# First batch in chunks of 64 tokens, and a pair's scores and sums in one block of products

## The chip, the cores and the metric

The kernel runs on one core of a Trainium2 chip. The metric is the time of one execution in device microseconds (us), as the median of five runs. All matrices are 32-bit floats; in the profile each product (matmul) leaves two records, with one weight load each.

## What is computed

Retention attention, then a two-layer network with a parametric ReLU:

```python
q, k, v: (8 batches, 8 heads, 576 tokens, 64)
scores = q @ k.T / sqrt(64)
Dmat = where(t >= s, gamma[h] ** (t - s), 0)      # gamma[h] = 1 - 2 ** (-5 - h)
ret = (scores * Dmat) @ v
x = ret as (8 * 576 tokens, 8 * 64)               # 4608 x 512
h = x @ w_in                                      # 512 x 2048
g = max(h, 0) + alpha * min(h, 0)
out = g @ w_out                                   # 2048 x 512
```

## The kernel before

Attention is computed in chunks. Within a chunk, the scores of each query with the keys are masked and multiplied with the values; all earlier chunks come in through a 64x64 matrix per head, the running sum of keys times values, which is multiplied with the queries ("the carried sums"). The powers of gamma are folded into scaled copies of q and v.

**The network** works on blocks of 256 tokens (`kb`) and units (`i`, eight per block, 256 of the 2048 hidden features each). Blocks 0 and 1 are "plain": `plain_unit` (L429) makes a unit's hidden values in the PSUM bank psh0, ACT takes them out with two ReLUs (L433, L435), DVE joins the two (L445, in `plain_relu`), and `plain_out` (L408, called by `mlp_out`) makes four products of 128x512 with w_out. `mlp_out` takes the oldest unit of the list `pend`; in the loop of the second batch that is the unit before. psh0 has one buffer, so the next L429 waits until L445 has read it. The later blocks (2 to 17) use a scheme with seven products in place of eight (`mlp_unit`, L473, and L391).

**The weights** come in 32 pieces of 512 KB, four per unit (two of w_in, two of w_out). `piece_in` takes a piece on ACT (L299, L301), `piece_out` works on it with three DVE operations (L310, L313, L315) and one on POOL (L317). Loads run ahead on SP's queue, limited by the bytes in flight (`load`, L78), and a loaded piece frees the buffer of a later one.

**The first batch** stands in three parts: tokens 0 to 255, 256 to 511 (the two large parts) and 512 to 575 (the last). For each large part, in this order: POOL scales q and v (`part_scale`, L678), TensorE transposes k and q (`part_transposes`, L698), then come the scores (`part_scores`, L719), the masks (`part_masks`: half of them one DVE operation, L729, the other half an ACT copy L731 and a POOL operation L732), the sums (`part_states`, L746; taken out by ACT L752 and POOL L754, or by DVE L756), the values and carried sums (`part_values`, L772 and L781), and ACT's copies to xb (L786). Chunks are 128 tokens long, two per part. Three products that nobody reads (`idle`, L849) follow the first part. The last part has its own functions (`last_transposes` L794, `last_scores` L803, `last_values` L814 and L821).

**The second batch** has four pairs of heads (n = 4 to 7), with nine chunks of 64. Its steps lie between the twelve plain units n = 0 to 11 that are left (i from 2 to 7, kb 0 and 1). `gap()` takes the next step at two places of a unit: ahead of `mlp_out`, and behind the second `piece_in`. The steps of a pair: "s" scores (`pair_scores`, L562, with masks L570 on DVE), "u" key-value products (`pair_states`, L580) with their running sums (`running_sums`, L589 on ACT, L591, L595, L597 on DVE), "w" their copies into the value tile (L603) and "p" the scaling of the next pair (L534 on POOL, L539 on ACT), "v" values (`pair_values`, L655, and ACT's L666) and "t" the next pair's transposes (L545 on DVE). `combine` adds weight sums on POOL (L327).

From L135 to L954 the order is the program's own (`tc.manual_schedule()`): each engine does its instructions in the order in which the code issues them. **The third batch and later** use `joint`: a pair's values are followed at once by `pair_front` for the next pair, which issues the scores (L619) and the key-value products (L625) as one block into two shared banks, and the ninth chunk's scores (L975) into a bank of its own, `extra`, masked by L632; the other masks are L639.

Of the kernel before, what the change touches and what calls it, by code (L numbers as in the profile page):

```python
# [14 lines left out]
ALU = mybir.AluOpType  # L15
# [3 lines left out]
def kernel(  # L19
# [121 lines left out]
    def room(i, s0, n):  # L141
# [8 lines left out]
        ((5, 4), (5, 5)), ((6, 5), (6, 6)))]  # L150
    carry = [None] + [room(i, 6, 1).rearrange("p (c d) -> p c d", d=D) for i in (2, 7)]

    def load_part(x):
        j0, j1 = PARTS[x]
        for i, src in ((0, k), (1, q), (2, v)):
            for m in range((j1 - j0 + 1) // 2):
# [5 lines left out]
                else:  # L162
# [20 lines left out]
    mask2 = const.tile([P, P], FP32, name="mask2")  # L183
    nc.gpsimd.memset(mask2, 1.0)
    nc.gpsimd.affine_select(out=mask2, in_=mask2, compare_op=ALU.is_ge, fill=0.0, base=0,
                            pattern=[[1, P]], channel_multiplier=-1)

    def mask(to):

        return mask2[to, to.start:to.stop]  # L190

# [208 lines left out]
    def plain_out(kb, i, g, between):  # L400
# [3 lines left out]
        for x in range(2):  # L404
            if x and between:
                between()
            for m in range(2):
                nc.tensor.matmul(acc[kb][m], g[:, 2 * x + m],  # L408
                                 w_out[i][:, 2 * x:2 * x + 2].rearrange("p x f -> p (x f)"),
                                 start=(i == 0 and x == 0), stop=(i == NU - 1 and x == 1))  # L410
# [140 lines left out]


    def pair_scores(n, kT, qT):
        c = pairs[n][1]

        mt = attn.tile([P, 2 * S], FP32, tag="at", name=f"mt_{n}").rearrange(
            "p (h j s) -> p h j s", h=2, s=C)
        ps = [ps_tile([P, NM, C], f"ps{p2}_{n}") for p2 in range(2)]
        for j in range(NJ):
            for h2 in range(2):  # L560
                x = (1 - h2, h2)[j % 2]
                nc.tensor.matmul(ps[j % 2][half(x), j // 2], kT[half(h2), chunk(j)],  # L562
                                 qT[half(h2), chunk(j)], start=True, stop=True)
        for h2 in range(2):
            nc.scalar.copy(mt[half(h2), h2].rearrange("p j s -> p (j s)"), qT[half(h2)])
        for p2 in range(2):
            for h2 in range(2):
                h, to, x = 2 * c + h2, half(1 - h2), (1 - h2, h2)[p2]
                nm = NM - p2
                nc.vector.scalar_tensor_tensor(  # L570
                    out=mt[to, h2, p2::2], in0=ps[p2][half(x), 0:nm], scalar=th[to, 3, h:h + 1],
                    in1=mask(to)[:, None, :].to_broadcast([C, nm, C]), op0=ALU.mult, op1=ALU.mult)
        return mt

    def pair_states(n, kn, vn):
        ps = [ps_tile([P, NM - 1, D], f"pu{p2}_{n}") for p2 in range(2)]
        for j in range(NJ - 1):
            for h2 in range(2):
                x = (h2, 1 - h2)[j % 2]
                nc.tensor.matmul(ps[j % 2][half(x), j // 2], kn[half(1 - h2), j],  # L580
                                 vn[half(1 - h2), h2, j], start=True, stop=True)
        return running_sums(n, *ps)

# [22 lines left out]

    later = []

    def pair_front(n, kT, qT, kn, vn, extra):
# [20 lines left out]
        for h2 in range(2):  # L630
            to = half(1 - h2)
            nc.vector.scalar_tensor_tensor(  # L632
                out=mt[to, h2, NJ - 1], in0=extra[to],
                scalar=th[to, 3, 2 * c + h2:2 * c + h2 + 1], in1=mask(to),
                op0=ALU.mult, op1=ALU.mult)
        for p2 in range(2):
            for h2 in range(2):
# [4 lines left out]
                    in1=mask(to)[:, None, :].to_broadcast([C, NM - 1, C]),  # L642
                    op0=ALU.mult, op1=ALU.mult)
        later.append(lambda: pair_sums(vn, running_sums(n, ps[0][:, 1], ps[1][:, 1])))
# [62 lines left out]

    def part_scores(x):
        at = tat[x] = [(mlp.tile([P, 8 * P], FP32, tag="g", name=f"pa{h2}_{x}") if x == 0 or h2
                        else room(4, 0, 4)).rearrange("p (c s) -> p c s", c=NPAIR)  # L710
                       for h2 in range(2)]
        banks = part_banks(x, 2 if x == 0 else None, "ps0"), part_banks(
            x, None if x == 0 else 0, "ps1")
        kT, qT = tT[x, 0], tT[x, 1]
        for m in range(2):
            to = slice(m * P, (m + 1) * P)
            for c in range(NPAIR):
                for h2 in range(2):
                    nc.tensor.matmul(banks[h2][m][:, c * P:(c + 1) * P], kT[half(h2), c, to],  # L719
                                     qT[half(h2), c, to], start=True, stop=True)  # L720
        return banks

    def part_masks(x, banks, h2):
        for m in range(2):
            to = tat[x][h2][:, :, m * P:(m + 1) * P]
            fro = banks[h2][m].rearrange("p (c s) -> p c s", c=NPAIR)
            w = mask2[:, None, :].to_broadcast([P, NPAIR, P])
            if h2 == 0:
                nc.vector.tensor_tensor(out=to, in0=fro, in1=w, op=ALU.mult)  # L729
            else:  # L730
                nc.scalar.copy(to, fro)  # L731
                nc.gpsimd.tensor_tensor(out=to, in0=to, in1=w, op=ALU.mult)  # L732

    def part_bank(x, n, b):
        return (ps_o.tile([P, 4 * P], FP32, tag=f"pso{n}", name=f"{b}_{x}") if n is not None else
                ps_a.tile([P, 4 * P], FP32, tag="psa", name=f"{b}_{x}"))


    def part_states(x):
        kn, vn = part[x][0], part[x][2]  # L740
        u = part_bank(x, 0 if x == 0 else None, "pu").rearrange("p (m c d) -> p m c d", m=2,
                                                                c=NPAIR)
        for m in range(2):
            for c in range(NPAIR):
                for h2 in range(2):
                    nc.tensor.matmul(u[half(h2), m, c], kn[:, m, 2 * c + h2],  # L746
                                     vn[:, m, 2 * c + h2], start=(m == 0 and c == 0),
                                     stop=(m == 1 and c == NPAIR - 1), skip_group_check=True)
        was = carry[x]
        for m in range(2):  # L750
            if x == 0:
                nc.scalar.copy(sums[x][m], u[:, m])  # L752
                if m:
                    nc.gpsimd.tensor_tensor(out=sums[x][m], in0=was, in1=sums[x][m], op=ALU.add)  # L754
            else:
                nc.vector.tensor_tensor(out=sums[x][m], in0=was, in1=u[:, m], op=ALU.add)  # L756
            was = sums[x][m]

    def part_carry(x):
        nc.gpsimd.tensor_tensor(out=carry[x + 1], in0=sums[x][1],  # L760
                                in1=gch[:, 2, :, None].to_broadcast([P, NPAIR, D]), op=ALU.mult)

    def part_values(x):
        vn, qT, at = part[x][2], tT[x, 1], tat[x]
        banks = [part_bank(x, (1, 2)[m] if x == 0 else (None, 2)[m], f"pv{m}").rearrange(
            "p (c s) -> p c s", c=NPAIR) for m in range(2)]
        xb[x] = ring.tile([P, NCC, TB], FP32, tag=f"x{x}", name=f"xb_{x}")
        su = [carry[x], sums[x][0]]
        for h2 in range(2):
            for m in range(2):  # L770
                for c in range(NPAIR):
                    nc.tensor.matmul(banks[m][half(h2), c], vn[:, m, 2 * c + h2],  # L772
                                     at[h2][:, c, m * P:(m + 1) * P], start=(c == 0),
                                     stop=(su[m] is None and c == NPAIR - 1),
# [266 lines left out]
```

## Time and profile before

| | |
|---|---|
| median of five runs | 1013.87 us (1013.28 to 1014.93) |
| profiled execution: its time | 1014.16 us |
| profiled execution: span, first to last instruction | 1012.5 us |
| TensorE (PE) busy | 1001.2 us, 99% |
| VectorE (DVE) busy | 775.4 us, 77% |
| ScalarE (ACT) busy | 265.9 us, 26% |
| GpSimd (POOL) busy | 179.9 us, 18% |
| TensorE clock granted over the span | 1.000 |
| DMA, mean | 63 GB/s, 230 GB/s in the first 60 us |

Times in views count from the first instruction of the profiled execution. A line of a timeline gives the start, the duration, the engine, the source line (L), the operation, the tiles written and read, the shapes, the number of records that were merged, and in brackets the idle time before it with what ended it. PEld is TensorE's weight loads. In the early stage (to about 60 us) all engines work at once; from about 17 us on TensorE has few gaps.

### The profile page before, as it was taken

Reading aid. Unit: us, or ns where it says so; the run is one execution under the profiler, and the core shown is the slowest. Engines: PE = TensorE matmul, PEld = TensorE weight load, DVE = VectorE, ACT = ScalarE, POOL = GpSimd, SP = SyncE. Lnnn points to the kernel's source line nnn. Section 1 sums busy time; section 2 is a strip of 40 time slices with the busy share of each in tenths; the row PEclk is TensorE's granted clock in tenths of the full one; section 3 lists DMA queues with packets and bytes.
Section 4 is the critical chain, followed back from the end, with each engine's and each line's share of the span. In section 5 each row is a group of like instructions: output and inputs, shape, how many; then the busy total and the mean of one; then the engine's idle time right before and its main releaser. Section 6 shows DMA issues by size and latency. Waiting matters only on the chain.

```text
span 1012.5 us, 22397 instructions
## 1 busy us (share of the span) xinstructions
PE 1001.2 (99%) x9023; PEld 897.4 (89%) x9023; DVE 775.4 (77%) x2086; ACT 265.9 (26%) x602; POOL 179.9 (18%) x200
## 2 busy tenths in 40 slices
PE   7999999999999999999999999999999999999998
PEld 6766668999999999999999999999999999999997
DVE  7669977987878878686877787878778776666665
ACT  4556653222222222022121222222222210000000
POOL 5646674310100020100011000200010001010000
PEclk9999999999999999999999999999999999999999
DMA  9974745332222313131121222323222000000000
GB/s 242 240 187 129 182 87 115 56 72 48 66 51 42 70 36 69 18 69 31 40 48 39 38 61 49 69 48 69 49 42 51 13 22 1 22 1 22 1 22 22
DMA packets 229592, 64.25 MB, mean 63 GB/s; under 512 B 214368, under 2 KB 223088, under 8 KB 229488
## 3 DMA queue, kind: packets, MB, share of 16 engines
q1 hardware_dynamic: 227088, 62.02, 27.2%
q8 instruction: 71, 1.16, 0.5%
q10 hardware_dynamic: 2400, 0.79, 0.4%
q14 instruction: 33, 0.27, 0.1%
HBM read 53.35 MB, written 9.44 MB: 62 GB/s over the span
## 4 chain that ended last, share of the span: by engine, by line
PE 98%; DMA 1%; POOL 0%; DVE 0%; ACT 0%; issue 0%; SPq 0%; DVEq 0%; POOLq 0%; ACTq 0%
PE ph L473 40%; PE po L391 38%; PE ph L429 6%; PE po L408 6%; PE pv L655 3%; PE ps L619 1%; PE ps L625 1%; DMA w_out<-in_k_dram 1%; PE pv L975 1%; PE ps L719 1%; PE pv L772 0%; PE pt L698 0%; PE pv L781 0%; PE ps L562 0%; PE idle L849 0%; POOL pa L732 0%
## 5 line engine op out<-in xcount | busy, mean ns | idle before, releaser
L391 PE MATMUL po<-w_out,g 128*128 128x256 f32 x1792 | 408.1, 379 | 0.0
L391 PEld LDWEIGHTS po<-w_out,g 128*128 128x128 f32 x1792 | 330.7, 190 | 39.7
L484 DVE TENSOR_TENSOR g<-ph,g 128x256 f32<-128x256 f32 (+1 forms) x512 | 187.5, 387 | 132.9 <-PE ph L473 67.0
L473 PE MATMUL ph<-xb,w_in 128*128 128x128 f32 x2048 | 272.7, 276 | 0.0
L473 PEld LDWEIGHTS ph<-xb,w_in 128*128 128x128 f32 x2048 | 257.1, 192 | 7.4 <-issue 0.5
L473 PE MATMUL ph<-xt,w_in 128*128 128x128 f32 x1536 | 213.3, 275 | 0.0
L473 PEld LDWEIGHTS ph<-xt,w_in 128*128 128x128 f32 x1536 | 192.1, 192 | 0.0
L479 ACT COPY g<-ph 128x128 f32<-128x128 f32 x128 | 34.0, 265 | 404.4 <-PE ph L473 397.8
L495 DVE TENSOR_TENSOR g<-g 128x128 f32<-128x128 f32 x512 | 130.5, 296 | 7.0
L534 POOL TENSOR_TENSOR qx<-qx,tabx 128x576 f32<-128x576 f32 x28 | 32.9, 1176 | 352.2 <-DMA qx<-in_q_dram 132.1
L489 DVE SCALAR_TENSOR_TENSOR g<-g 128x512 f32<-128x512 f32 x128 | 89.9, 702 | 3.0
L487 DVE TENSOR_SCALAR g<-g,alpha 128x256 f32<-128x256 f32 x256 | 85.8, 377 | 3.6
L408 PE MATMUL po<-w_out,g 128*128 128x512 f32 x128 | 58.6, 599 | 0.9 <-DVE g L445 0.9
L429 PE MATMUL ph<-xb,w_in 128*128 128x256 f32 x256 | 58.6, 383 | 0.0
L666 ACT COPY xb<-pv 128x256 f32<-128x256 f32 (+3 forms) x84 | 23.1, 314 | 126.5 <-PE pv L655 126.5
L429 PEld LDWEIGHTS ph<-xb,w_in 128*128 128x128 f32 x256 | 47.9, 190 | 9.3 <-issue 2.4
L603 ACT COPY vn<-su 64x512 f32<-64x512 f32 x56 | 34.5, 616 | 78.8 <-DVE su L597 78.5
L639 DVE SCALAR_TENSOR_TENSOR mt<-ps,th,mask 64x256 f32<-64x256 f32 x96 | 46.4, 483 | 2.2
L459 POOL TENSOR_TENSOR xt<-xb 128x256 f32<-128x256 f32 x16 | 11.6, 726 | 195.9 <-PE ph L473 195.9
L408 PEld LDWEIGHTS po<-w_out,g 128*128 128x128 f32 x128 | 23.4, 190 | 24.5 <-issue 21.8
L632 DVE SCALAR_TENSOR_TENSOR mt<-pv,th,mask 64x64 f32<-64x64 f32 x48 | 13.6, 283 | 40.1 <-ACT xb L666 39.7
L539 ACT ACTIVATE vn<-vn,tabv 64x576 f32<-64x576 f32 x56 | 43.3, 772 | 1.3
(135 smaller groups left out, 750.6 us busy)
## 6 DMA issues: line engine op xcount, KB each, us to landing
out_dram<-osb SPq DMA_DIRECT2D x34, 256.0 KB, 2.1
kx<-in_k_dram SPq DMA_DIRECT2D x112, 72.0 KB, 2.5
qx<-in_q_dram SPq DMA_DIRECT2D x112, 72.0 KB, 2.9
vn<-in_v_dram SPq DMA_DIRECT2D x56, 144.0 KB, 3.2
kn<-in_k_dram SPq DMA_DIRECT2D x56, 144.0 KB, 3.6
raw<-in_moe_w_in_dram SPq DMA_DIRECT2D x24, 256.0 KB, 4.2
raw<-in_moe_w_out_dram SPq DMA_DIRECT2D x10, 512.0 KB, 4.3
w_in<-in_moe_w_out_dram SPq DMA_DIRECT2D x6, 512.0 KB, 5.0
```

The lines of the kernel that those rows point to most:

```text
L391: nc.tensor.matmul(acc[kb][n // 2][:, n % 2, :], g[:, x, :], w_out[i][:, y, :], start=(i == 0 and n % 2 == 0), stop=(i == NU - 1 and (n % ...
L408: nc.tensor.matmul(acc[kb][m], g[:, 2 * x + m], w_out[i][:, 2 * x:2 * x + 2].rearrange("p x f -> p (x f)"), start=(i == 0 and x == 0), sto ...
L429: nc.tensor.matmul(ph[:, x], w_in[i // UST][:, cc // 2 * 2 + x, i % UST, cc % 2], xb[kb][:, cc], start=(cc == 0 and x == 0), stop=(cc == N ...
L473: nc.tensor.matmul(ph[m][:, o], w_in[i // UST][:, l, i % UST, cc], r[:, cc], start=(n in (0, 3) and cc == 0), stop=(n in (2, 6) and cc == ...
L479: nc.scalar.copy(g[:, 7], ph[0][:, 2])
L484: nc.vector.tensor_tensor(out=o, in0=x0, in1=x1, op=ALU.add)
L487: nc.vector.tensor_scalar(g[:, 4 + 2 * m:6 + 2 * m], g[:, 2 * m:2 * m + 2], 0.0, alpha[:, fc:fc + 1], ALU.min, ALU.mult)
L489: nc.vector.scalar_tensor_tensor(out=g[:, 0:4].rearrange("p x t -> p (x t)"), in0=g[:, 0:4].rearrange("p x t -> p (x t)"), scalar=0.0, in1 ...
L495: ins = nc.vector.tensor_tensor(out=g[:, o, :], in0=g[:, x0, :], in1=g[:, x1, :], op=op)
L539: nc.scalar.activation(vn[x, h2], vn[x, h2], ACTF.Copy, scale=tabv[x, c:c + 1])
L603: nc.scalar.copy(vn[half(h2), h2, 1:], su[half(h2)])
L639: nc.vector.scalar_tensor_tensor(out=mt[to, h2, p2:NJ - 1:2], in0=ps[p2][half(x), 0], scalar=th[to, 3, h:h + 1], in1=mask(to)[:, None, :]. ...
```

## The change

Two things change.

**First batch.** The two large parts are computed in chunks of 64 tokens, four per part. Scores go into two banks in place of four, one for each head of a pair, and with half as many elements to mask: for the first part all by DVE, for the second all by ACT and POOL. There are four running sums per part in place of two. All products are 64 deep, where those for sums and values were 128 deep; the carried sums are made 32 columns wide. After the first part, two unread products follow in place of three.

**Second batch.** `pair_scores` and `pair_states` go. The scores and key-value products of a pair are one block from `pair_front`, as in the later batches, issued inside `mlp_out` of the units n = 2, 4, 7 and 9, between the third and the fourth of the second product's four matmuls; `piece_out` then follows `mlp_out` in place of preceding it. The ninth chunk's scores go to a tile in psh0. The running sums follow at the end of the same unit, and the copies, the values and the next pair's steps in the next unit.

```diff
-    sums = ... ((5, 4), (5, 5)), ((6, 5), (6, 6)))]
+    sums = ... ((5, 4), (5, 5), (5, 6), (6, 4)), ((6, 5), (6, 6), (7, 4), (7, 5)), ())]
...
-    mask2 = const.tile([P, P], FP32, name="mask2")          # one affine_select
+    mask = const.tile([P, C], FP32, name="mask")            # two, one for each 64 partitions
...
         for x in range(2):
-            if x and between:
-                between()
             for m in range(2):
+                if between and 2 * x + m == between[0]:
+                    between[1]()
                 nc.tensor.matmul(acc[kb][m], g[:, 2 * x + m],
...
+    def last_chunk(n, extra):
+        kT, qT = turned[n]
+        for h2 in range(2):
+            nc.tensor.matmul(extra[half(1 - h2)], kT[half(h2), chunk(NJ - 1)],
+                             qT[half(h2), chunk(NJ - 1)], start=True, stop=True)
...
-        later.append(lambda: pair_sums(vn, running_sums(n, ps[0][:, 1], ps[1][:, 1])))
+        later.append(lambda: running_sums(n, ps[0][:, 1], ps[1][:, 1]))
...
     def part_scores(x):
+        banks = part_banks(x, 2 if x == 0 else None, "ps")
+        for m in range(2):
+            for c in range(NPAIR):
+                for p2 in range(2):
+                    for h2 in range(2):
+                        j = chunk(2 * m + p2)
+                        nc.tensor.matmul(banks[h2][half(p2), (2 * c + m) * C:(2 * c + m + 1) * C],
+                                         kT[half(h2), c, j], qT[half(h2), c, j],
+                                         start=True, stop=True)
+        for h2 in range(2):
+            ...
+            if x == 0:
+                nc.vector.tensor_tensor(out=to, in0=fro, in1=m, op=ALU.mult)
+            else:
+                nc.scalar.copy(to, fro)
+                nc.gpsimd.tensor_tensor(out=to, in0=to, in1=m, op=ALU.mult)
...
     def part_states(x):
+                        nc.tensor.matmul(banks[p2][half(h2), m, c], kn[half(p2), m, 2 * c + h2],
+                                         vn[half(p2), m, 2 * c + h2], ...)
+        for j in range(4):
+            u = banks[j % 2][:, j // 2]
+            if x == 0:
+                nc.scalar.copy(sums[x][j], u)
+                if j:
+                    nc.gpsimd.tensor_tensor(out=sums[x][j], in0=was, in1=sums[x][j], op=ALU.add)
+            else:
+                nc.vector.tensor_tensor(out=sums[x][j], in0=was, in1=u, op=ALU.add)
+            was = sums[x][j]
...
     def part_values(x):
+                        nc.tensor.matmul(banks[p2][half(h2 ^ p2), c, m],
+                                         vn[half(p2), m, 2 * c + h2],
+                                         at[half(p2), h2, n * C:(n + 1) * C], ...)
+        for j in range(1 if x == 0 else 0, 4):
+            su = sums[x][j - 1] if j else carry[x]
+            for c in range(NPAIR):
+                for h2 in range(2):
+                    for e in range(0, D, 32):
+                        to = (h2 ^ (j % 2)) * D + e
+                        nc.tensor.matmul(banks[j % 2][to:to + 32, c, j // 2],
+                                         su[half(h2), c, e:e + 32], qT[half(h2), c, chunk(j)], ...)
+        for c in (slice(0, 2), slice(2, 4)) if x == 0 else (slice(0, NPAIR),):
+            nc.scalar.copy(to[:, 0, c], banks[0][:, c])
+            for h2 in range(2):
+                nc.scalar.copy(to[half(h2), 1, c], banks[1][half(1 - h2), c])
...
-    for _ in range(3):
+    for _ in range(2):
         nc.tensor.matmul(idle, ident, part[0][0][:, 0].rearrange("p h d -> p (h d)"),
...
-        elif what == "s":
-            mts[n] = pair_scores(n, *turned.pop(n))
         elif what == "u":
-            sus[n] = pair_states(n, loaded[n][0], loaded[n][3])
+            sus[n] = later.pop(0)()
...
+    def amid(n):
+        extra = ps_h.tile([P, C], FP32, tag="psh0", name=f"pe_{n}")
+        last_chunk(n, extra)
+        pair_front(n, *turned.pop(n), loaded[n][0], loaded[n][3], extra)
...
-    steps = [(("t", NPAIR),)]
-    for n in range(NPAIR, last + 1):
-        steps += [(("s", n),), (("u", n),), (("w", n), ("p", n + 1)), (("v", n), ("t", n + 1)), ()]
+    before, after, fronts = {1: (("t", NPAIR),)}, {0: (("p", NPAIR),)}, {}
+    for n, at in zip(range(NPAIR, last + 1), (2, 4, 7, 9)):
+        fronts[at] = n
+        after[at] = (("u", n),)
+        before[at + 1] = (("w", n), ("p", n + 1))
+        after[at + 1] = (("v", n), ("t", n + 1))
...
         plain_unit(kb, i)
         plain_relu()
-        if n >= 1:
-            gap()
+        for x in before.pop(n, ()):
+            step(*x)
         piece_in(1)
-        piece_out(1)
-        mlp_out()
-        if n == 0:
-            step("p", NPAIR)
+        if n in fronts:
+            mlp_out((3, lambda: amid(fronts[n])))
+            piece_out(1)
+        else:
+            piece_out(1)
+            mlp_out()
         combine(1)
         piece_in(1)
-        if n >= 2:
-            gap()
+        for x in after.pop(n, ()):
+            step(*x)
         piece_out(1)
         combine(2)
```

In the later batches, `pair_sums` is now called by the loop that pops `later`, with the running sums that it returns; the products, their order and the masks' shapes stay as they are.

## The prediction

> **What bounds the kernel now.** First the chain that ended last, by engine, then the same chain in order of time (start us, us, what; in a record count, one product is two records).
>
> ```profile
> PE 98%; DMA 1%; POOL 0%; DVE 0%; ACT 0%; issue 0%; SPq 0%; DVEq 0%; POOLq 0%; ACTq 0%
> ```
>
> ```profile
> 18.75 2.77 PE idle L849 x6
> ...
> 31.69 1.99 PE ps L719 x32
> 33.68 0.04 issue
> 33.72 1.15 PE pu L746 x32
> ...
> 38.52 3.26 PE pv L772 x32
> 41.78 1.90 PE pv L781 x32
> ...
> 56.27 0.58 PE pv L821 x32
> ...
> 74.26 3.45 PE ph L429 x16
> 77.71 0.73 PE ps L562 x36
> 78.44 3.63 PE po L408 x8
> 82.07 0.62 PE pu L580 x32
> 82.70 3.65 PE ph L429 x16
> 86.35 3.43 PE po L408 x8
> ...
> 162.52 0.46 PE ps L619 x27
> 162.98 0.47 PE ps L625 x32
> ```
>
> TensorE sets the time: its work and its few waits are what can change. Three prices stand here. A block of 64x64x64 products that uses all four quarters of the array costs 0.47 us for 32 records, 14.7 ns each (L625). Going from full products to such a block costs about 0.2 us (L562: 36 records would be 0.53, it takes 0.73), and going back another 0.20 (L408 takes 3.63 instead of 3.43). Blocks that use two tiles of the array are slower: L746 takes 36 ns a record, L781 59 ns, L772 102 ns.
>
> Then the timeline around one pair of the second batch, for the engine that could become late:
>
> ```profile
> 78.87 0.87 DVE L445 SCALAR_TENSOR_TENSOR g<-g,nalpha,ph 128x256 f32<-128x256 f32 x2 [0.36 <-ACT ph L435]
> 79.78 2.13 DVE L570 SCALAR_TENSOR_TENSOR mt<-ps,th,mask 64x320 f32<-64x320 f32 x4
> 81.83 0.68 DVE L310 TENSOR_SCALAR wc<-wa 128x512 f32<-128x512 f32 x1
> ...
> 88.77 0.87 DVE L445 SCALAR_TENSOR_TENSOR g<-g,nalpha,ph 128x256 f32<-128x256 f32 x2
> ...
> 96.19 0.86 DVE L445 SCALAR_TENSOR_TENSOR g<-g,nalpha,ph 128x256 f32<-128x256 f32 x2
> ```
>
> DVE works almost without a gap from 78.87 to 104. An L445 without a bracket started straight after the instruction before it, so DVE is the late one there. L445 frees the bank psh0 of a plain unit; before, only the next unit's L429 needs that bank, a whole second product later.
>
> **Part A: the first batch in chunks of 64.** Second large part (tokens 256 to 511), on TensorE. Old: 1.99 + 1.15 + 3.26 + 1.90 = 8.30 us (L719, L746, L772, L781). New: 64 records of scores and 64 of sums at 14.7 ns, 1.88; 64 of values, 0.94; 128 of the carried sums, 32 wide. Those are nearest to L821 (32 records in 0.58, 18 ns): 1.9 at 14.7 ns, 2.3 at 18. Two entries of 0.2. Together 5.1 to 5.5, so 2.8 to 3.2 us less.
>
> First large part. The weight load of L719 drops from 330 to 188 ns at 12.4 us: the array runs at half speed until then. Scores, 64 records at 29 ns, run 10.05 to 11.95; sums, 15 records at 29 ns and 49 at 14.7, to 13.15. The masks are now two DVE operations (0.72 each), 12.05 to 13.5; before, POOL L732 (2 x 1.26) ended at 16.59 and TensorE waited for it. Values 13.55 to 14.65; the carried sums, 96 records, to 16.2; they need L754's sums, three POOL additions of 0.65 after ACT's copies, ready at 14.2, 14.85 and 15.5. Two unread products (four records of 0.43) end at 18.0, alpha's transpose at 18.2. The third one is no saving of its own: before, the three filled the time until weight piece 1 came (POOL L317, 19.70 to 21.00).
>
> Which pieces does the first unit need? Its first half needs piece 0, its second piece 1. ACT took piece 0 at 14.44, behind the two L731 copies; these copies go, the bytes land at 11.6 (issued 7.52, 4.1 us), so DVE has it at 13.5, POOL is done at 17.3, and piece 1 follows at 19.15. The copies of xb (now six, 2.0 us) end at about 18.8. L429 can start at 18.3 instead of 21.68. If the clock stays at half speed through the whole part, TensorE gets there at 20.9.
>
> What is late next? Not the unit, but POOL before L794. Piece 6 lands at 29.5 (issued 23.86, 5.6 us), which no faster engine changes; ACT 0.6, DVE 30.1 to 32.3; four L756 (0.43 each, two before) to 34.0; DVE's piece 7 to 36.2, POOL's to 37.5; one L678 of 1.02 to 38.6, which the second half of L794 needs. TensorE would be there at 37.6 to 38.0, so it waits 0.6 to 1.0, and L408 after it starts at 39.2 instead of 44.32. The gain is **5.1 us**, whether L429 started at 18.3 or 19.2. If it started at 20.9, TensorE itself is last and the gain is 3.7. Of the extra instructions, ACT's two more copies for the first part's sums and POOL's two more additions (1.3 us) lie under pieces that wait for DVE; the three copies of L786's place (0.6 us more) lie before L803, which comes a whole L408 (3.6 us) later. No DMA is added, and SP's order and limit of bytes in flight stay. The second mask select (0.29 like L185) lies on POOL before 5.49, where POOL waits for DVE. From 45 to 72 us DVE idles (5.98 before L806, 4.90 before an L445), so the second batch starts with nothing owed.
>
> **Part B: the block amid the second product.** Saved for each pair: one of two entries and one of two returns, 0.73 + 0.20 + 0.62 + 0.20 = 1.75 against 1.19 + 0.20 (the block at 162.3, which has the same products). 0.36 us, four pairs, **1.44**.
>
> Added: the ninth chunk's scores go to psh0, so the block waits for L445 of its own unit, three products (2.57 us) after that unit's L429 ended. Behind it in TensorE's queue stand the whole block, the fourth product and the next unit. On DVE, L632 and L639 wait for the block, and behind them stand two weight pieces, the sums L591 to L597 and the next L445. By the rows of pair 4, on the clock of before:
>
> Unit 2: L429 ends at 77.71, three products later it is 80.3; L445 ended at 79.74, no wait. But DVE now stands still from 79.74 to 80.5, and L632 and L639 (0.58 + 1.99 at 163) are 0.4 longer than L570. DVE is at piece 17 at 83.0 instead of 81.83, and nothing gives this back up to the next L445, which ends at 90.8 instead of 89.64. TensorE, 0.36 early, wants psh0 for unit 4 at 90.6: **0.3** wait. Unit 4: L445 ended at 97.05 and now, about as late, at 98.0; TensorE is at the block at 90.9 + 3.65 + 2.57 = 97.1: **0.9** wait. The same lateness before units 6 and 7 costs **0.4** and **0.7** (two L545 now stand before unit 6's pieces, and unit 6 has no step in which TensorE is busy elsewhere). Unit 6 lets DVE catch up, so unit 7's block waits for nothing; units 7 to 9 repeat units 2 to 4 (**0.3**, **0.9**). After unit 9 the weight pieces are used up. The values of pairs 5 and 7, and SP's loads behind them, come half a unit earlier; that moves nothing else, since the loads land (2.5 to 3.6 us) units before their use. Together 3.5, less 1.44: **2.1 us slower**. The bounds: no wait at all, 1.4 us faster; a wait of 1.2 us at each of the four blocks, 3.4 slower. I take 2.1, since the gapless DVE rows leave little room.
>
> **Weighed.** The Trainium skill, TensorE: Matmul & The Clock Gate, section "Wait — 56ns, not 53.3ns?", says that products never start less than about 25 ns apart however small they are. L619 and L625 show 14.7 ns a record, so the rows decide; by the page, the 608 records of part A would take 6.3 us longer, and the sum would be 3.5 us slower than before.
>
> **The sum.** The joint blocks of the later batches keep their products. 5.1 - 2.1 = 3.0 us off; I keep 0.2 back for the copy that L794 now has to wait for (its buffer psa is that of the values): 2.8. The profiled execution took 1014.16 (span 1012.5, 1.66 around it), so 1011.4 for one like it; the median of the runs is 0.29 lower, so 1011.1.
>
> **Rivals.**
> 1. The block costs no wait (DVE gets ahead, or psh0 is free early): 5.1 + 1.4 off, 1007.4. For it, L445 of unit 2 is free in time; against it, the unbracketed L445 at 88.77 and 96.19. Chance 0.12.
> 2. Part A gives only 2.8 to 3.7: the array stays at half speed through the first part (3.7), or the first part gains nothing and the second only its own 2.8. That makes 1012.3 to 1013.2, no difference. For it, the DMA queues are full until 45 us, and the full clock came only at 12.4. Against it, the new blocks leave TensorE fewer gaps before that. Chance 0.27.
> 3. Slower: the small products of part A do not issue at 14.7 ns. The nearest slower row with the same operands is L746 (36 ns). From 19.3 ns a record the 608 records eat the whole 2.8 us, from 22.6 ns the kernel is slower by over 0.2%; halfway between the two rows (25.4 ns) it takes about 1017.6. For it, the first part's operands lie in w_out tiles as L746's do; against it, L625 has the same shapes, at 14.7. Chance 0.09.
> 4. The change does not join the blocks, since psh0 holds it up: then DVE's lateness is the forecast's own 3.5 us, so this is inside it.
>
> **How the numbers follow.** The forecast has 0.52: 1011.1, its own range 1009.8 to 1012.5. About 0.2% (2.0 us) is what a measurement of this kernel can tell from no change. Faster by over that: rival 1 and most of the forecast, 0.56. Within: the rest of the forecast and rival 2, 0.34. Slower: rival 3 and a worse part B, 0.10. The range reaches from between the forecast and rival 1, 1008.7, to the end of rival 2 with some of the worse waits, 1014.3.
>
> **What would show it.** Right: scores and sums of the second large part in about 2.0 us and its values in 1.1; L429 of the first unit before 19.5; L408 after L794 near 39.2, with L794 waiting for POOL L678; one small block per pair of 1.2 us between L408 records; TensorE waits of 0.3 to 0.9 for DVE L445 at units 4, 6, 7 and 9. Wrong: these waits missing, L772's place above 20 ns a record, or weight loads of 330 ns after 13.5 us.

## The result and the profile after

The changed kernel takes 1015.68 us (median of 24 runs, 1013.86 to 1021.07), the kernel before 1014.02 in the same comparisons (42 runs, 1012.96 to 1015.36). The ratio is 1.0021, interval 1.0015 to 1.0027: slower, by a little, where 1011.1 was forecast. The profiled execution took 1016.72 (span 1015.0).

First where the time went. In the changed kernel L426 is the old L429, L405 the old L408, L442 the old L445, L470 the old L473. The block is L578 (the ninth chunk's scores), L591 (scores) and L597 (key-value products), with the masks L604 and L611; L555 to L561 are the running sums, L567 ACT's copies of them, L627 the values. The second batch's first L426 starts at 57.51 us (60.32 before), and the first L470, which ends that stage, at 158.07 (155.54 before). So the first batch gained 2.8 us and the second lost 5.3 (100.56 us in place of 95.22). From there to the end both kernels take 856.9 us.

The page's line of the chain that ended last, and the start of that chain in order of time:

```profile
PE 85%; DVE 0%; ACT 0%; DVEq 0%; issue 0%; ACTq 0%
```

```profile
148.69 0.62 ACT vn L567
...
150.00 1.15 PE pv L627 x30
```

Before, TensorE held 98% of the chain. The 85% means only that the view follows the chain back to 148.6 us and no further: there TensorE's values L627 waited for ACT's copies L567 of the last pair's running sums into the value tile. The prediction has no such wait.

TensorE's waits from 60 to 165 us (us in total, times, longest):

```profile
PE ph L426 <- DVE g L442: 2.1, 4, 0.9
PE pe L578 <- DVE g L442: 1.3, 2, 0.7
PE pv L627 <- ACT vn L567: 1.0, 3, 0.4
```

The first two were forecast, 3.5 us in six places: they are 3.4 in six places (0.45, 0.64, 0.44, 0.85, 0.35, 0.70). The third was not, and its 1.0 us hides more. TensorE's timeline from the values of two pairs to the next unit (start, duration):

```profile
86.54 1.61 PE L627 MATMUL pv<-mt,vn 128*64 128x64 f32 x36
88.60 3.69 PE L426 MATMUL ph<-xb,w_in 128*128 128x256 f32 x16 [0.45 <-DVE g L442]
...
148.63 0.34 PE L627 MATMUL pv<-mt,vn 128*64 128x64 f32 x4
...
150.00 1.15 PE L627 MATMUL pv<-mt,vn 128*64 128x64 f32 x30 [0.31 <-ACT vn L567]
151.08 1.13 PE L426 MATMUL ph<-xb,w_in 128*128 128x256 f32 x4
```

Before, 1.20 us passed from the first values of a pair to the next full product, at every pair. Now it is 1.61, 2.15, 1.61 and 2.45 us (L426's own wait taken off): 3.0 us more. The short stops inside L627 are too small to be listed as waits, so the list shows a third of them. At the first and third pair (1.61) the values keep their place among the units; at the second and fourth (2.15, 2.45) they stand half a unit earlier than before. Why the copies are late stands in DVE's timeline around the first pair, the same place that the prediction shows of before:

```profile
76.06 0.87 DVE L442 SCALAR_TENSOR_TENSOR g<-g,nalpha,ph 128x256 f32<-128x256 f32 x2 [0.37 <-ACT ph L432]
77.79 0.58 DVE L604 SCALAR_TENSOR_TENSOR mt<-pe,th,mask 64x64 f32<-64x64 f32 x2 [0.86 <-PE pe L578]
78.73 1.99 DVE L611 SCALAR_TENSOR_TENSOR mt<-ps,th,mask 64x256 f32<-64x256 f32 x4 [0.36 <-PE ps L597]
80.64 0.68 DVE L307 TENSOR_SCALAR wc<-wa 128x512 f32<-128x512 f32 x1
...
83.82 1.46 DVE L559 SCALAR_TENSOR_TENSOR su<-su,gch 128x64 f32<-128x64 f32 x3
85.20 0.41 DVE L561 SCALAR_TENSOR_TENSOR su<-su,gch,ps 128x192 f32<-128x192 f32 x1
```

DVE stands still for 0.86 and 0.36 us because its queue holds only the block's masks next; then a weight piece (2.1 us) goes ahead of the running sums, which end at 85.6; ACT's copies run from 85.70 to 86.96, and the values began at 86.54.

In the first batch the saving is there but smaller. TensorE and ACT in the changed kernel (start, duration):

```profile
14.76 0.42 PE L748 MATMUL pv<-pT,w_out 64*32 64x64 f32 x14
16.41 1.21 PE L748 MATMUL pv<-pT,w_out 64*32 64x64 f32 x82 [1.23 <-issue]
...
36.23 1.16 PE L737 MATMUL pv<-w_out,w_out 64*64 64x64 f32 x62 [0.59 <-POOL w_out L699]
...
40.32 0.46 PE L764 MATMUL pt<-ident,w_out 64*128 64x64 f32 x4 [1.30 <-ACT xb L754]
...
41.43 3.70 PE L405 MATMUL po<-w_out,g 128*128 128x512 f32 x8
```

```profile
31.89 0.68 ACT L296 ACTIVATE wa<-raw 128x512 f32<-128x512 f32 x1 [3.17 <-DMA raw<-in_moe_w_out_dram]
...
33.02 1.05 ACT L698 COPY w_out<-ps 128x512 f32<-128x512 f32 x2
...
38.56 0.68 ACT L296 ACTIVATE wa<-w_in 128x512 f32<-128x512 f32 x1 [2.07 <-DVE w_out L312]
...
39.70 0.56 ACT L754 COPY xb<-pv 128x512 f32<-128x512 f32 x1
```

Three new stops. The carried sums L748 halt for 1.2 us for nothing that the profile shows. The second part's values L737 wait 0.6 us for POOL's masks (L699), which follow ACT's copies L698, and ACT takes piece 6 only at 31.9 (29.5 was forecast). The last transposes L764 wait 1.3 us for ACT's copy L754, which stands behind piece 8. (The view names DVE L312 for ACT's wait at 38.56, but L312 ends at 38.57; the second half of piece 8, issued at 30.49, lands at 38.46.) L405 starts at 41.43 instead of the forecast 39.2.

### The profile page after: what moved, and what is told of

Read it like the earlier page. It is cut to its first block, busy times and chain, and to the rows that moved or that the text cites. A ratio compares the mean times of both kernels' runs of the same rounds, so it can differ in the third digit from the quotient of the medians.

```text
span 1015.0 us, 23128 instructions
## 1 busy us (share of the span) xinstructions
PE 996.2 (98%) x9389; PEld 892.6 (88%) x9389; DVE 776.1 (76%) x2094; ACT 267.4 (26%) x605; POOL 178.9 (18%) x201
## 3 DMA queue, kind: packets, MB, share of 16 engines
q8 instruction: 74, 1.21, 0.5%
## 4 chain that ended last, share of the span: by engine, by line
PE 85%; DVE 0%; ACT 0%; DVEq 0%; issue 0%; ACTq 0%
PE ph L470 40%; PE po L388 38%; PE pv L627 3%; PE ps L591 1%; PE ps L597 1%; PE po L405 1%; PE pv L578 1%; PE ph L426 0%; ACT vn L567 0%; DVE s L367 0%; DVE u L367 0%; DVE osb L367 0%; DVE osb L368 0%; DVEq L1007 0%; ACTq L567 0%
## 5 line engine op out<-in xcount | busy, mean ns | idle before, releaser
L388 PEld LDWEIGHTS po<-w_out,g 128*128 128x128 f32 x1792 | 330.7, 190 | 39.7
L470 PE MATMUL ph<-xb,w_in 128*128 128x128 f32 x2048 | 272.7, 276 | 0.0
L470 PEld LDWEIGHTS ph<-xb,w_in 128*128 128x128 f32 x2048 | 257.1, 192 | 7.4 <-issue 0.5
L470 PE MATMUL ph<-xt,w_in 128*128 128x128 f32 x1536 | 213.3, 275 | 0.0
L470 PEld LDWEIGHTS ph<-xt,w_in 128*128 128x128 f32 x1536 | 192.1, 192 | 0.0
L426 PE MATMUL ph<-xb,w_in 128*128 128x256 f32 x256 | 58.4, 382 | 2.1 <-DVE g L442 2.1
L405 PE MATMUL po<-w_out,g 128*128 128x512 f32 x128 | 59.1, 598 | 0.4 <-DVE g L442 0.4
L426 PEld LDWEIGHTS ph<-xb,w_in 128*128 128x128 f32 x256 | 48.0, 190 | 12.7 <-issue 4.0
L611 DVE SCALAR_TENSOR_TENSOR mt<-ps,th,mask 64x256 f32<-64x256 f32 x112 | 54.1, 483 | 3.9 <-PE ps L597 1.5
L567 ACT COPY vn<-su 64x512 f32<-64x512 f32 x56 | 34.6, 617 | 79.9 <-DVE su L561 79.5
L604 DVE SCALAR_TENSOR_TENSOR mt<-pv,th,mask 64x64 f32<-64x64 f32 x48 | 13.6, 283 | 40.2 <-ACT xb L638 39.8
L627 PEld LDWEIGHTS pv<-mt,vn 128*64 128x64 f32 x1008 | 32.5, 138 | 12.9 <-DVE g L492 7.6
```

What stands on the lines that cost most here:

```text
L388: nc.tensor.matmul(acc[kb][n // 2][:, n % 2, :], g[:, x, :], w_out[i][:, y, :], start=(i == 0 and n % 2 == 0), stop=(i == NU - 1 and (n % ...
L405: nc.tensor.matmul(acc[kb][m], g[:, 2 * x + m], w_out[i][:, 2 * x:2 * x + 2].rearrange("p x f -> p (x f)"), start=(i == 0 and x == 0), sto ...
L426: nc.tensor.matmul(ph[:, x], w_in[i // UST][:, cc // 2 * 2 + x, i % UST, cc % 2], xb[kb][:, cc], start=(cc == 0 and x == 0), stop=(cc == N ...
L470: nc.tensor.matmul(ph[m][:, o], w_in[i // UST][:, l, i % UST, cc], r[:, cc], start=(n in (0, 3) and cc == 0), stop=(n in (2, 6) and cc == ...
L567: nc.scalar.copy(vn[half(h2), h2, 1:], su[half(h2)])
L611: nc.vector.scalar_tensor_tensor(out=mt[to, h2, p2:NJ - 1:2], in0=ps[p2][half(x), 0], scalar=th[to, 3, h:h + 1], in1=mask[to, None, :].to_ ...
```

## The experiments

Each result is a median, beside runs of the kernel before on the same chip (1013.8 to 1013.9 us).

**The two parts alone.** The first kernel has the changed first batch and the old steps of the second, the second kernel the reverse:

```diff
-        if n in fronts:
-            mlp_out((3, lambda: amid(fronts[n])))
-            piece_out(1)
-        else: ...
+        if n >= 1:
+            gap()                      # "s", "u", "w" "p", "v" "t" as before
+        piece_in(1); piece_out(1); mlp_out()
```

> Only the first batch is changed (chunks of 64, two unread products); the second batch is that of before. Theory: the first batch gains, by the profile of after 60.32 - 57.51 = 2.8 us at the start of the second batch's first unit, and in executions whose loads land earlier up to the 5.1 of the prediction; so 1009 to 1011.2, and a spread of more than 2 us between executions. Rival: the first batch gains nothing in the median and only the profiled execution shows 2.8: 1013 to 1015.

> Only the second batch is changed (the block inside the second product); the first batch is that of before. Theory: the second batch loses 5.3 us (86.8 us from unit 2 to the first unit of block 2, where before took 81.4), whatever the first batch does: 1019 to 1020, with a spread as small as that of before. Rival: the loss comes from the first batch arriving earlier while the weights do not, so that the second batch meets late pieces: then this kernel loses 2 us or less, 1014 to 1016.

First batch alone: 1011.08 us (1010.13 to 1012.01), ratio 0.9971 (0.9960 to 0.9982). Second alone: 1019.11 (1018.53 to 1019.70), ratio 1.0052 (1.0039 to 1.0065). So 2.8 us gained and 5.2 lost, both as expected and in agreement with the two stretches of the trace. (The spread of the first is 1.9 us where over 2 was expected. The sum, 2.4 us slower, lies between the medians' difference of the whole change, 1.7, and that of the two profiled executions, 2.6.) The second kernel shows the three waits of the changed kernel again, to the digit (2.1, 1.3 and 1.0 us).

**The order of piece and block.** Only the second batch is changed; DVE gets its weight piece ahead of the block's masks.

```diff
         if n in fronts:
-            mlp_out((3, lambda: amid(fronts[n])))
             piece_out(1)
+            mlp_out((3, lambda: amid(fronts[n])))
```

> As the kernel with only the second batch changed, but in the units with a block the weight piece is worked on ahead of the second product and its block, as in before, so that DVE has work while TensorE comes to the block. Theory (DVE stands still for about 0.9 + 0.4 us before the masks at each block, and this lateness reaches the next units' banks and the running sums): most of the 5.3 us goes, 1014.5 to 1016.5, and the waits of L429 for L445 two units later shrink to under 0.3. Rival (the wait of the block for its own unit's L445, or the longer masks, cost the time): nothing changes within 1 us, 1018.5 to 1020.

1014.36 us (1013.36 to 1015.3), ratio 1.0005 (0.9996 to 1.0014): 4.75 us of the 5.2 are gone, slightly more than expected. DVE's timeline at the same place:

```profile
80.07 0.69 DVE L310 TENSOR_SCALAR wc<-wa 128x512 f32<-128x512 f32 x1
...
82.24 0.58 DVE L607 SCALAR_TENSOR_TENSOR mt<-pe,th,mask 64x64 f32<-64x64 f32 x2
82.86 1.99 DVE L614 SCALAR_TENSOR_TENSOR mt<-ps,th,mask 64x256 f32<-64x256 f32 x4
...
85.78 0.93 DVE L564 SCALAR_TENSOR_TENSOR su<-su,gch 128x64 f32<-128x64 f32 x3
```

The piece fills the time in which DVE stood still, and the masks start without a bracket. TensorE's only listed wait in this stage is 0.6 us for the mask L607, which now frees psh0 late; by the starts the products around the four blocks lose 1.6 us to it. From the values to the next product it is 1.19 to 1.30 us again.

**The running sums alone.** As the second batch alone, but with the sums directly behind the masks.

```diff
             mlp_out((3, lambda: amid(fronts[n])))
+            for x in after.pop(n):      # ("u", n)
+                step(*x)
             piece_out(1)
```

> First batch as before, second batch as changed, but DVE's running sums of a pair stand directly behind the masks, ahead of the weight piece that follows the second product, instead of behind it. Theory (of the 5.2 us that the second batch lost, 2.8 are values that wait for the copies of the running sums, and these were late only because a piece of 2.1 us stood ahead of them on DVE; the other waits come from DVE's late L445, which has the same work ahead of it in either order): values take 1.3 us again, L429 and the block still wait about 3.4 us for L445, and the time is 1016.3 us (1015.5 to 1017.2) where the changed order gave 1019.1. Rival (the values' waits are only a form of DVE's lateness, which comes back as a longer wait for L445): 1018.5 to 1019.5. Second rival (the late block alone costs nothing): 1014.4 as with the piece ahead of the block.

1016.01 us (1015.54 to 1018.03), ratio 1.0025 (1.0016 to 1.0034): 3.1 us less than in the changed order, as expected. All four L630 take 1.27 us, and none waits. DVE does the same work before each L445, so those waits stay:

```profile
PE ph L429 <- DVE g L445: 2.0, 4, 1.1
PE pe L581 <- DVE g L445: 0.6, 1, 0.6
PE pe L581 <- ACT mt L604: 0.5, 1, 0.5
```

The values' wait is thus a loss of its own, beside DVE's late L445.

**The first batch's parts.** Only the first large part in chunks of 64, the second in 128 as before:

```diff
-    part_scores(1)
+    banks = part_scores_128(1); part_masks_128(1, banks, 0); part_masks_128(1, banks, 1)
...
-    part_states(1); part_values(1); part_carry(1)
+    part_states_128(1); part_values_128(1); part_carry_128(1)
```

> The first batch as changed only in its first large part (tokens 0 to 255 in chunks of 64); the second large part is in chunks of 128 as before, and so is everything behind it. Theory (the first batch is set by when piece 6 lands and by what ACT, DVE and POOL then do in order, not by TensorE): the 3 us that TensorE saves in the second part only turned into the waits seen with both parts (0.2 for POOL, 1.6 for ACT's copy L785), so the first part alone is worth nearly all: 1011.1 to 1012.0 us against 1011.1 with both, and TensorE has no wait over 0.3 us between the first L426 and the last transposes. Rival (the parts add up, as the forecast had them on TensorE): the second part is worth its 2.8 us less the 1.8 us of waits and more, the first part alone 1012.8 or later. Second rival (the first part is worth nothing, since the first unit waits for its weights): 1013.9.

1012.26 us (1011.9 to 1013.91): between the expectations, a miss for both. The first part is worth about 1.7 us, the second about 1.2, though it takes 3 us off TensorE. In this kernel TensorE has no wait from 30 us to the last transposes, and the second product behind them starts at 42.47, against 42.06 with both parts, which lose 1.8 us to waits (0.2 for POOL, 1.6 for ACT). So the second part's saving was mostly turned into waits, but not all of it.

**ACT, then ACT and POOL.** In the first kernel ACT takes piece 6 behind the copies of the second part's scores, and piece 8 behind the last transposes:

```diff
-    piece_in(1)
     part_scores(1)
+    piece_in(1)
...
-    piece_in(1)
     part_values(1)
...
     last_transposes()
+    piece_in(1)
```

In the second kernel only piece 8 is moved, and the last part's scaling goes ahead of pieces 6 and 7 on POOL:

```diff
+    part_scale(2, 1)
+    part_scale(2, 2)
     plain_unit(0, 1)
     piece_out(1)
-    part_scale(2, 1)
     plain_relu()
-    piece_in(1)
     part_values(1)
-    part_scale(2, 2)
     part_carry(1)
     last_transposes()
+    piece_in(1)
```

> As the kernel with only the first batch changed, but ACT takes piece 6 after the second part's score copies and piece 8 after the values' copies and the last part's transposes, so that no copy stands behind a load that has not landed. Theory (late pieces 6 and 8 hold up ACT, and so the masks, the values and L794): about 1.5 to 2.5 us faster than the kernel with only the first batch changed, and a smaller spread. Rival (the weights of the next unit are themselves too late): no gain or a loss, since the second product then waits for pieces 6 and 7.

> The first batch as changed, the second as before, and two moves in the first batch: the last part's scaling of q and k on POOL (L681) goes ahead of weight pieces 6 and 7, and ACT takes piece 8 behind the last transposes instead of ahead of the copies L785. Theory (in order: piece 6 lands, ACT, DVE, POOL, and the last transposes stand behind both ACT's and POOL's pieces): the transposes follow the carried sums by 0.3 us instead of 1.6, L405 behind them starts 1.3 us earlier, and the time is 1009.8 us (1009.2 to 1010.5) where the first batch alone gave 1011.1. Rival (another wait takes its place: L405 for piece 6 or 7, now later on POOL): 1011.1 and a wait of L405 for POOL L314 of 1 us.

With ACT alone: 1012.56 us (1010.75 to 1014.52), no gain on 1011.08, and a wider spread. The rival's sign is missing too: its second products wait for no piece. Its profiled execution has a stop of 2.1 us in the carried sums and is 2.1 us later at the first L426, but the order can be read: the transposes wait 0.27 us for ACT and then 0.92 for POOL, which was next in line. With both: 1009.74 (1008.78 to 1011.67), ratio 0.9963 (0.9951 to 0.9975), as expected 1.3 us below the first batch alone; the transposes wait 0.36 us, and L405 follows at 41.72, though this execution came to its first L426 only at 21.93.

**The stop in the carried sums.** The two unread products go between the values and the carried sums of the first part.

```diff
+        if x == 0:                      # in part_values, ahead of the carried sums
+            idle = ps_h.tile([P, DM], FP32, tag="psh0", name="idle")
+            for _ in range(2): ...
-    idle = ...                          # behind part_values(0)
```

> The first batch as changed, the second as before; the two unread products (2.0 us) are moved from behind the carried sums of the first part to between its values and its carried sums. In the three profiles of the changed first batch the carried sums stop after 14 records for 1.2 to 2.1 us, and TensorE goes on 2.2 to 2.4 us after a packet of 16 KB on the instruction queue has started. Theory (TensorE runs out of instructions, since it uses up small products faster than they are brought): the unread products take 2 us in which the next instructions come, so the stop goes or falls under 0.4 us, the first L426 starts 1 to 1.5 us earlier than 19.5, and the time stays within 0.5 us of 1011.1, since piece 6 sets the rest. Rival (the stop belongs to the carried sums: to the tile of sums or to the half-wide products): it stays at 1.2 us or more after 14 records of L779.

```profile
14.71 1.98 PE L776 MATMUL idle<-w_out,ident 128*128 128x512 f32 x4
16.63 1.40 PE L784 MATMUL pv<-pT,w_out 64*32 64x64 f32 x96
...
32.76 0.27 PE L740 MATMUL pu<-w_out,w_out 64*64 64x64 f32 x2 [1.81 <-issue]
32.96 5.41 PE L426 MATMUL ph<-xb,w_in 128*128 128x256 f32 x16
```

1010.14 us (1008.64 to 1014.49), ratio 0.9966 (0.9956 to 0.9977). The stop in the carried sums is gone: 96 records in 1.40 us, and the first L426 starts at 18.90, 0.6 us earlier than with the first batch alone (19.49); 1 to 1.5 was expected, but 0.72 us ahead of this L426 go to nothing that the profile shows. The time was expected within 0.5 us of 1011.1 and is 0.9 below it. The rival, that the stop belongs to the carried sums themselves, is out. Nor was an operand late: the first 32 of these records read only the first running sum, which ACT had copied by 13.92 in the changed kernel (first L717), and the stop came after 14. A similar stop stands at the last two records of the second part's sums L740; three other profiles have one in the same place (0.24, 0.30 and 1.26 us).

**Put together.** The whole change with the piece ahead of the block, then the first batch with all three moves, then both batches with everything:

> The whole change, first and second batch, but with the weight piece ahead of the second product as before, so that DVE has it before it stands still for the block. Theory (the two parts only add up, and the order of piece and block is the whole loss): 1011.1 for the first batch and 0.5 for the second batch in this order, 1011.6 us (1011.0 to 1012.2), with one wait of TensorE for the masks of 0.6 us in the second batch. Rival (the second batch, which begins 2.8 us earlier, finds DVE or the loads further behind): 1012.6 or more, with L426 waits for DVE L442.

> First batch as changed, second as before, with three moves in the first batch together: the last part's scaling ahead of pieces 6 and 7 on POOL, ACT's piece 8 behind the last transposes, and the two unread products between values and carried sums of the first part. Theory (the first two take away the wait of the last transposes, worth 1.3 us; the third only takes away the stop in the carried sums, and with it the half clock behind it, worth 0.9 as measured): 1008.8 us (1008.2 to 1009.8), and where a stop stays it is later, at the last two sums of the second part. Rival (the two gains are one and the same, since both only bring TensorE to the same landing of piece 6): 1009.7.

> The whole change with the piece ahead of the block in the second batch and the three moves in the first. Theory (second batch in this order costs about 0.4 us against the old one, the rest adds up): 1009.2 us (1008.5 to 1010.2). Rival (TensorE comes to the second batch earlier than DVE has the weights ready): 1010.5 or more, with waits of L426 for DVE or ACT after 57 us.

| kernel | us | ratio to before |
|---|---|---|
| both batches, piece ahead of the block | 1011.44 (1009.67 to 1013.05) | 0.9973 (0.9962 to 0.9983) |
| first batch, three moves | 1008.66 (1008.11 to 1009.96) | 0.9952 (0.9940 to 0.9965) |
| both batches, all moves | 1010.61 (1008.98 to 1011.38) | 0.9968 (0.9955 to 0.9980) |

The first two came as expected. One exchanged pair of calls turns the change from 1015.68 to 1011.44. The first batch alone with its moves is the best version found, 5.1 us under the kernel before. In the last kernel the profile shows 0.6 us for the masks L604, and 1.6 us for POOL's masks in the first batch (L737 behind L699), so its distance of 1.4 us from the expected 1009.2 is not settled. Its rival has the number (1010.5 or more), but the 0.6 us are also in the kernel of the first row. The smaller differences between these kernels (0.9 and 1.3 us for single moves) are medians of five to nine runs with overlapping ranges.

## Why the prediction was wrong

- **The second batch, the step that failed.** The prediction says that the values of pairs 5 and 7 come half a unit earlier and that "that moves nothing else, since the loads land". (The second batch was to lose 2.1 us; it lost 5.2.) It checked the loads and left out the running sums, on which the values of every pair depend. These stood behind the block's masks and a weight piece. Counted from the start of the unit with the block, at pairs 4 and 6 they ended 1.6 and 1.7 us later than before, which cost 0.4 us each; at pairs 5 and 7 the values came 3.1 and 3.0 us earlier and the sums only 1.5 and 0.9, which cost 0.95 and 1.25. That is 3.0 us in the trace, 3.1 in the experiment, and the larger part of the miss.
- **The saving was right.** 0.36 us a pair was forecast. Unit 2 has a block that waits for nothing (first the kernel before, then the changed one):

```profile
74.10 3.62 PE L429 MATMUL ph<-xb,w_in 128*128 128x256 f32 x16
...
82.63 3.72 PE L429 MATMUL ph<-xb,w_in 128*128 128x256 f32 x16
86.19 3.60 PE L408 MATMUL po<-w_out,g 128*128 128x512 f32 x8
```

```profile
71.28 3.62 PE L426 MATMUL ph<-xb,w_in 128*128 128x256 f32 x16
...
79.56 3.62 PE L426 MATMUL ph<-xb,w_in 128*128 128x256 f32 x16
83.02 3.60 PE L405 MATMUL po<-w_out,g 128*128 128x512 f32 x8
```

By their starts, a full L429 takes 3.45 us and a full L408 3.43 where only full products stand around them. Before, unit 2 took 8.53 to the next L429, and that one 3.56 to its L408: 1.75 more than the full products, as forecast. Now it takes 8.28, and the next L426 3.45: 1.39 more, as forecast.
- **The waits for L445 were right** in size and place: at unit 4 0.45 and 0.64 (forecast 0.3 and 0.9), units 6 and 7 0.44 and 0.85 (0.4 and 0.7), unit 9 0.35 and 0.70 (0.3 and 0.9); together 3.4 against 3.5. By the starts, which also count what a stop costs the products around it, they are 3.75. With the values' 3.0 and the saving of 1.4 that is the 5.3 us of the trace.
- **The first batch, a mis-sized term.** 5.1 forecast, 2.8 measured. The price of the products held: scores and sums of the second part 2.03 us (forecast 2.0), values 1.08 (1.1), carried sums 1.71 (1.9 to 2.3), and L426 came at 19.68 (18.3 to 19.2). What failed is the step "Piece 6 lands at 29.5 (issued 23.86, 5.6 us), which no faster engine changes": in the changed kernel's profile it landed at 31.8, 7.1 us after its issue, and L405 came 2.2 us after the forecast. The 5.6 was one execution's landing: in the four profiles with the first batch of before this load took 5.1, 5.6, 5.8 and 7.8 us, in the nine with a changed one 5.1 to 7.9. The prediction followed POOL behind that piece and forgot ACT, whose queue holds the masks' copies behind piece 6 and the copies L754 behind piece 8. Moving the work of ACT and POOL from behind the pieces gave 1.3 us, taking the stop out of the carried sums 0.9, and both 2.4: with them the first batch gains 5.1 us, which is what the forecast gave it, but in another order of work: that the numbers agree is chance.
- **The rivals.** The slower one was in its right direction for a wrong reason. Small products did not become slower: 128 records of carried sums in 1.71 us are 13.4 ns each, far from the 19.3 at which that rival starts. Counted by records, that is also below the 25 ns between the starts of products that the Trainium skill names (TensorE: Matmul & The Clock Gate, "Wait — 56ns, not 53.3ns?"); counted by products, of two records each, the mean is 26.7 ns and is not. The second (a first batch worth 2.8 to 3.7) holds by its number, for that batch alone; its reasons, half clock in the first part or no gain there, were not what the trace shows.

## What to carry to other kernels

When a step is moved earlier on one engine, list everything that it reads and look up where each producer now stands in its own queue; a load that has landed says nothing about a sum that another engine still has to make. If an engine must wait for a block, put independent work ahead of that wait in its queue, not behind it: here one exchanged pair of calls was worth 4.2 us. And a landing time read from one execution is not a constant (here 5.1 to 7.9 us for one load), so an engine that works in order should not have urgent copies behind a load.

## What the hardware showed

**TensorE stops in a long run of small products.** In six profiles with the unread products behind the carried sums, TensorE halts after exactly 14 records of them, for 1.2 to 2.4 us, without a wait that the profile shows. In each a packet of 16 KB on the instruction queue starts at most 1.2 us ahead of the halt, and TensorE went on 2.2 to 2.4 us after its start (packet at 14.0, on at 16.41 in the changed kernel; 14.4 and 16.79; 14.8 and 17.16). The kernel before has such a packet at 15.9 and no stop: its products there take 110 ns a record (L772 of the first part, 32 records in 3.53 us) in place of 15. That TensorE runs out of instructions while the queues are full (mean DMA share 0.95 in the first 60 us) is the reading that fits, and two slow products in that place took the stop away. The packet does not name its engine, and the later stops at L740 end 2.6 to 3.3 us after such a packet's start (29.6 and 32.76 in the profile shown above), so it stays an inference.

**A longer stop costs the clock.** After stops up to 1.78 us the granted clock stays 1.00 and the remaining 82 records take 1.21 us. After 2.10 and 2.39 us they take 1.72 and 1.91. After the 1.81 us in the profile shown above, sixteen L426 records take 5.41 us in place of 3.72, with the granted clock at 0.50 from 34 to 37 us. In each of these three profiles the half clock lasts 3.41 us and begins 0.1 to 1.2 us after the stop's end. The Trainium skill (TensorE: Matmul & The Clock Gate, "What's actually happening") has the clock fall after at least one idle window of about 3.4 us; here 1.81 us without a product was enough, and the measurement decides. With 1.78 and 1.81 us on the two sides, whether the length alone decides is not shown. The half clock goes with the upper end of the changed kernel's spread: the six of its 24 runs with a mean granted clock of 0.996 to 0.998 took 1016.51 to 1021.07 us, the other eighteen 1013.86 to 1017.23. A mean of 0.996 over 1019 us is about 4 us of lost clock (an estimate from these figures), so it is not the whole spread of 7 us.

**DVE's small additions wait for POOL's.** The three operations of 128x64 in the running sums (L559) take 1.46, 2.00, 1.46 and 2.37 us at the four pairs of the changed kernel while POOL adds (L314, L324), and 0.93 us (L564 of the piece ahead of the block) when POOL is idle. One of them takes 0.285 us with POOL idle; one that begins while a POOL addition runs ends 0.08 us after that addition does, and so takes up to 1.19 us beside one L324 of 1.27 us.
